# The first expert slots' table moved into the second to last head pair, and the last pair's adds moved to VectorE

## The chip, the cores and the metric

The kernel runs on one core of one Trainium2 chip. The metric is the device time of one execution, in microseconds (us). The engines are TensorE (PE in the rows, its weight loads PEld), VectorE (DVE), ScalarE (ACT), GpSimd (POOL) and SyncE (SP), which issues most of the DMA transfers. GpSimd issues the indirect transfers (gathers and scatters).

## What is computed

Attention in which a query sees only keys of its own hash bucket (the signs of six projections), and then a mixture of experts with one expert for each token:

```python
scores = scale * np.matmul(q, k.transpose(0, 1, 3, 2))      # B=4, H=8, S=768, D=64
scores = np.where(q_bucket[..., None] == k_bucket[..., None, :], scores, -1e9)
attn = np.exp(scores - scores.max(-1, keepdims=True))
attn = attn / (attn.sum(-1, keepdims=True) + 1e-09)
x = np.matmul(attn, v).transpose(0, 2, 1, 3).reshape(3072, 512)
logits = x @ w_gate + modality_bias[modality_id]            # 8 experts
e_idx = np.argmax(logits, axis=1)
gate_w = softmax(logits)[np.arange(N), e_idx]
for e in range(8):
    mask = e_idx == e
    out[mask] = gate_w[mask, None] * (np.maximum(x[mask] @ w1[e], 0) @ w2[e])
```

## The kernel before

Attention is worked in 16 pairs of heads, i = 0 to 15; four pairs make a batch. A pair has six tiles of 128 keys, kt = 0 to 5. TensorE's instructions stand in the order in which the program's text issues them. That order is written out by hand as strings, one string for each kt: PLAN0 for pair 0, LAST for pair 15 and PLAN for the pairs between. The other engines' order comes from a scheduler. The letters that matter here:

- S is a score step: matmuls of L410 and L411, one exponential on ScalarE (L430 or L444) into a tile `pb`. After the last step of a key tile kt > 0 two adds (L447), one for each head h, sum the weights up in `sp`. They are GpSimd's, but in pair 15 those of h = 1 are VectorE's (CFG's `spd`).
- A weighs the values: 16 matmuls of L463 for two key tiles. Pair i's last A leaves its sums of all keys in `ut`.
- Q calls `sums(i - 1)`: eight matmuls (L486) that sum the previous pair's `sp` over the keys, and a copy or add of VectorE into `gs` (L489, L491). The adds of all six key tiles of pair i - 1 must be done for it. "sums(14)" below is the Q in pair 15. sums(15) is called by `finish(3)`, among the first matmuls of the experts.
- M prepares the next pair's masks (L344, L350 on TensorE, reduced on VectorE by L346, L352), T turns and takes signs of the pair after that (L220; VectorE's masks L231 and then L312), v sums the values up on GpSimd (`va`, L384 to L386).
- x and y take a step of `finish_x`: a tile of the last finished batch's x is transposed (four matmuls, L548), scaled on VectorE into `xs` (L550, two buffers) and stored to `x_d` in HBM by SP (L552). f, F, e and E are steps of `finish`, which divides by the sums, routes the tokens and has GpSimd scatter their numbers into the table `tab` in HBM (L784). For the third batch this scatter, six indirect transfers, runs in pairs 13 and 14.

The first expert block that is worked is known once three batches are routed. `early_slots` finds on VectorE where it lies (some 20 tiny instructions and `eslot`). SP reads `eslot` into a register and loads the rows `tb` of the table (L941). GpSimd makes `at` from them (L947) and gathers the tokens' x with four indirect transfers into `xg` (L949). TensorE transposes `xg` (L967, eight matmuls for the first two chunks of 128 columns, eight for the others), ScalarE copies (`xh`, L970), VectorE subtracts (`xl`, L974), and the first layer's matmuls `hps` start (L985 with `xh`, L986 with `xl`, L987 with `xh`, for each of four chunks c). The weights come as `raw`, ScalarE rounds them (`w`, L929), and VectorE or, for every second one of the first eight, GpSimd makes the rest (`w`, L933). The first eight transposes stand on TensorE behind pair 15's second A, the other eight behind its third.

Of the kernel before, what the change touches and what calls it, by code (L numbers as in the profile page):

```python
# [30 lines left out]
P = 128  # L31

GROUP = 2
PLAN = (
    "yMSTSTMSM",
    "STEeLfvxMAVSSMMTxfe",
    "eySMSMlARRQfMSFMyF",
    "SRMSeMSMx",
# [13 lines left out]
    "SevAVSSe",  # L52
    "eySSAQSy",
    "SSeS",
# [39 lines left out]
def attention(ctx, actx, tc, a, x_d, l_d, route=None, setup=None, before_last=None):  # L94
# [318 lines left out]
    def score(i):  # L413

        t = st[i]
        t["sp"] = spool.tile([P, 2, S], F32, name="sp")
        t["pb"] = [pbuf[(NT * i + kt) % NPB] for kt in range(NT)]

        banks = [0]

        def bank(shape):
            banks[0] += 1
            if i == NPR - 1 and banks[0] % 2:
                return ps_m.tile(shape, F32, name="psm")
            return ps_s.tile(shape, F32, name="pss")

        def main(kt, h):
            sp = bank([P, MAIN])
            scores(t, sp, h, kt, COLS[0])
            marks["p"] = nc.scalar.activation(t["pb"][kt][:, h, 0:MAIN], sp, AF.Exp, scale=0.125).ins  # L430

        if i == 0:
            for kt in range(NT):
                main(kt, 0)
                yield
        for kt in range(NT):
            pb = t["pb"][kt]
            for h in range(int(i == 0), 2):
                main(kt, h)
                yield  # L440
            sp = bank([P, 2, REST])
            for h in range(2):
                scores(t, sp[:, h], h, kt, COLS[1])
            nc.scalar.activation(pb[:, :, MAIN:S], sp, AF.Exp, scale=0.125)  # L444
            if kt > 0:
                for h in range(2):
                    marks["add"] = (nc.vector if h and i in CFG["spd"] else nc.gpsimd).tensor_tensor(out=t["sp"][:, h], in0=(t["pb"][0] if kt == 1 else t["sp"])[:, h], in1=pb[:, h], op=ALU.add).ins  # L447
            yield
# [137 lines left out]
    with tc.manual_schedule(engines={mybir.EngineType.PE}):  # L586
# [23 lines left out]
        for i in range(NPR):  # L610
# [8 lines left out]
            for kt in range(NT):  # L619
                if i == NPR - 1 and kt == 1:  # L620
                    before_last(ps_x.tile([P, MAIN], F32, name="psx"))
                if i == NPR - 1 and kt < 3:
                    next(xs, None)
                    next(xs, None)
                for c in (PLAN0 if i == 0 else LAST if i == NPR - 1 else PLAN)[kt]:
# [15 lines left out]
                    elif c == "V":  # L641
                        vsums(i)
                    elif c == "Q":
                        if i > 0:
# [4 lines left out]
                    elif c == "l":  # L649
                        if i + 1 < NPR:  # L650
                            load_v(i + 1)
                    elif c == "F" and i % 4 == 0 or c == "f" and i % 4 == 1:
                        next(fins, None)
                    elif c == "e" and i % 4 >= 2 or c == "E" and i == NPR - 2:
                        next(fins, None)
                    elif c == "x" and i % 4 == 2 or c == "y" and i % 4 == 3:
                        next(xs, None)
                        next(xs, None)
# [36 lines left out]
def router(ctx, tc, a, x_d, tab):  # L695
# [136 lines left out]

    def early_slots(sp):
        out = const.tile([P, 2, EARLY], I32, name="eslot")
# [50 lines left out]
def experts(ctx, tc, a, x_d, tab, out, ps_x, idents, fold, marks):  # L885
# [66 lines left out]
    def xprep(s, xg, dst):  # L952
# [11 lines left out]
        for c in range(4):  # L964
# [6 lines left out]
            if s == ("e", 0) and c == 1:  # L971
                after(marks["U", 4], tr.ins)
                after(marks["ut"], cp.ins)
            nc.vector.tensor_tensor(out=xl[:, c, 0:SL], in0=tp[:, 0:SL], in1=xh[:, c, 0:SL].bitcast(F32), op=ALU.subtract)  # L974
            if c % 2:
# [221 lines left out]
def body(tc, a, out):  # L1197
# [4 lines left out]
    with ExitStack() as ctx, ExitStack() as actx:  # L1202
        route, early_slots, late_slots, setup = router(ctx, tc, a, x_d, tab)
        finish, finish_x, ps_x, idents, fold, marks = attention(ctx, actx, tc, a, x_d, None, route, setup, lambda sp: eslot.append(early_slots(sp)))
        actx.close()
# [40 lines left out]
```

## Time and profile before

| | us |
|---|---|
| median of three runs | 759.83 (759.24 to 761.26) |
| the profiled execution, its own time | 760.22 |
| its span, first to last instruction | 758.1 |
| TensorE busy in it | 738.9 |
| VectorE, GpSimd, ScalarE busy | 499.9, 440.9, 363.8 |

The profiled execution is one run of the program. Its own time is 2.1 us longer than its span, and 0.39 us longer than the median. Pair 14 runs from about 411 to 430 us in it, pair 15 to 458 us, and the experts from there to the end.

### The profile page before, as it was taken

What the parts mean: (1) busy time and instruction counts of PE and PEld (TensorE: products, weight loads), DVE (VectorE), ACT (ScalarE), POOL (GpSimd) and SP (SyncE); (2) the same over time, 40 slices, a digit from 0 to 9 for tenths busy, and PEclk for the clock granted to TensorE, in tenths of its full rate; (3) what the DMA queues carried; (4) which work ended last, traced back from release to release, by engine and by line L of the source; (5) the groups of instructions that cost most, each with busy time, mean ns of one, the idle gap of its engine ahead of it and who ended that gap; (6) DMA issues with size and microseconds to landing.
All of it is one profiled execution on the core that took longest, in us unless ns stands there. A gap on an engine that the chain in (4) does not pass through costs nothing.

```text
span 758.1 us, 12219 instructions
## 1 busy us (share of the span) xinstructions
PE 738.9 (97%) x4308; PEld 523.4 (69%) x4308; DVE 499.9 (66%) x878; ACT 363.8 (48%) x649; POOL 440.9 (58%) x339
## 2 busy tenths in 40 slices
PE   6899999999999999999999999999999999999995
PEld 3556576566666657666666656888888877788884
DVE  6997779789877887977987877654343442334423
ACT  5446565555555555556465454343343432424333
POOL 8598779769888769887869984712222202202011
PEclk9999999999999999999999999999999999999998
DMA  9464455345676435664324163556544764434332
GB/s 187 116 142 109 113 122 140 83 106 116 111 131 162 105 91 133 121 157 124 92 69 85 61 199 112 115 207 185 159 137 139 250 214 147 141 123 139 96 113 82
DMA packets 105832, 99.26 MB, mean 131 GB/s; under 512 B 62594, under 2 KB 82978, under 8 KB 105760
## 3 DMA queue, kind: packets, MB, share of 16 engines
q1 hardware_dynamic: 99616, 83.79, 43.6%
q0 software_dynamic: 4832, 12.94, 4.9%
q10 hardware_dynamic: 1312, 1.65, 0.9%
q8 instruction: 36, 0.59, 0.4%
q14 instruction: 36, 0.29, 0.2%
HBM read 59.33 MB, written 12.94 MB: 95 GB/s over the span
## 4 chain that ended last, share of the span: by engine, by line
PE 81%; issue 9%; DMA 3%; POOL 2%; SPq 1%; DVE 1%; ACT 1%; POOLq 0%; ACTq 0%
PE psu L463 17%; PE pss L410 9%; PE pss L411 8%; PE psm L344 5%; PE hps L985 5%; PE hps L986 5%; PE hps L987 5%; PE yps L1026 4%; PE yps L1027 4%; PE yps L1028 4%; PE psm L350 3%; PE psx L303 2%; PE psx L486 2%; PE psx L548 2%; PE psu L220 1%
## 5 line engine op out<-in xcount | busy, mean ns | idle before, releaser
L447 POOL TENSOR_TENSOR sp<-sp,pb 128x768 f32<-128x768 f32 x124 | 225.3, 1851 | 14.1 <-ACT pb L444 13.4
L346 DVE TENSOR_REDUCE mx<-psm 128x1 f32<-128x512 f32 x192 | 130.0, 687 | 22.2 <-PE psm L344 19.1
L430 ACT ACTIVATE pb<-pss 128x512 f32<-128x512 f32 x186 | 111.5, 600 | 58.7 <-PE pss L411 50.2
L463 PE MATMUL psu<-pb,vt 128*64 128x512 f32 (+1 forms) x768 | 136.1, 497 | 0.0
L933 DVE TENSOR_TENSOR w<-raw,w 128x1024 fp32r<-128x1024 f32 x52 | 66.9, 1287 | 97.9 <-ACT w L929 97.3
L463 PEld LDWEIGHTS psu<-pb,vt 128*64 128x64 f32 x768 | 51.3, 137 | 70.6 <-issue 60.9
L929 ACT CAST w<-raw 128x1024 fp32r<-128x1024 f32 x56 | 58.5, 1047 | 81.4 <-PE yps L1028 76.7
L444 ACT ACTIVATE pb<-pss 128x512 f32<-128x512 f32 x93 | 55.6, 598 | 82.3 <-PE pss L411 80.0
L1096 POOL DMA_INDIRECT out<-y,tb x25 | 24.6, 984 | 104.1 <-ACT y L1095 100.4
L447 POOL TENSOR_TENSOR sp<-pb,pb 128x768 f32<-128x768 f32 x31 | 56.2, 1835 | 45.2 <-ACT pb L444 45.2
L1026 PE MATMUL yps<-w,hl 128*128 128x512 f32 x200 | 79.5, 397 | 0.0
L1027 PE MATMUL yps<-w,hh 128*128 128x512 f32 x200 | 78.1, 391 | 0.0
L1028 PE MATMUL yps<-w,hh 128*128 128x512 f32 x200 | 78.0, 390 | 0.0
L949 POOL DMA_INDIRECT xg<-x_d,tb x17 | 18.4, 1084 | 98.1 <-DMA tb<-tab 94.4
L985 PE MATMUL hps<-xh,w 128*128 128x496 f32 x192 | 74.4, 388 | 0.0
L986 PE MATMUL hps<-xl,w 128*128 128x496 f32 x192 | 73.8, 384 | 0.0
L987 PE MATMUL hps<-xh,w 128*128 128x496 f32 x192 | 73.8, 384 | 0.0
L410 PE MATMUL pss<-m_0g,s_0g 128*128 128x512 f32 (+1 forms) x186 | 69.2, 372 | 0.0
L991 DVE SCALAR_TENSOR_TENSOR hl<-hps,hh 128x496 fp32r<-128x496 f32 x48 | 32.4, 674 | 53.0 <-ACT hh L990 52.9
L352 DVE TENSOR_REDUCE mx<-psm 128x2 f32<-128x512 f32 x96 | 66.1, 688 | 1.0
L410 PE MATMUL pss<-m_1g,s_1g 128*128 128x512 f32 (+1 forms) x186 | 65.7, 353 | 0.2 <-ACT pb L430 0.2
L990 ACT ACTIVATE hh<-hps 128x496 fp32r<-128x496 f32 x48 | 28.1, 585 | 78.5 <-PE hps L987 76.1
(267 smaller groups left out, 1419.7 us busy)
## 6 DMA issues: line engine op xcount, KB each, us to landing
raw<-moe_w SPq DMA_DIRECT2D x56, 512.0 KB
vt<-v SPq DMA_DIRECT2D x16, 384.0 KB
qk<-q SPq DMA_DIRECT2D x31, 192.0 KB
qk<-k SPq DMA_DIRECT2D x31, 192.0 KB
x_d<-xs SPq DMA_DIRECT2D x18, 256.0 KB
tw<-moe_w SPq DMA_DIRECT2D x2, 2048.0 KB
m_0g<-m_0g SPq DMA_DIRECT2D x16, 192.0 KB
s_0g<-s_0g SPq DMA_DIRECT2D x16, 192.0 KB
```

The source lines that it names most:

```text
L346: marks["m"] = nc.vector.tensor_reduce(out=mx[:, qt + j, hi, 0:1], in_=mp, axis=AX.X, op=ALU.max).ins
L410: nc.tensor.matmul(out, t["s1"][h][:, ks], t["m1"][h][:, cs], start=True, stop=False)
L430: marks["p"] = nc.scalar.activation(t["pb"][kt][:, h, 0:MAIN], sp, AF.Exp, scale=0.125).ins
L447: marks["add"] = (nc.vector if h and i in CFG["spd"] else nc.gpsimd).tensor_tensor(out=t["sp"][:, h], in0=(t["pb"][0] if kt == 1 else t["s ...
L463: marks["u", kt] = nc.tensor.matmul(t["u"][part][64 * h:64 * h + 64, 0:w], t["v"][:, h, kt], t["pb"][kt][:, h, COLS[part]], start=False, s ...
L933: (nc.gpsimd if n < 8 and n % 2 else nc.vector).tensor_tensor(out=lo, in0=r, in1=hi.bitcast(F32), op=ALU.subtract)
L985: nc.tensor.matmul(hps, lo[:, c, fs], xh[:, c, 0:SL], start=(c == 0), stop=False)
L986: nc.tensor.matmul(hps, hi[:, c, fs], xl[:, c, 0:SL], start=False, stop=False)
L987: nc.tensor.matmul(hps, hi[:, c, fs], xh[:, c, 0:SL], start=False, stop=(c == 3))
L1026: nc.tensor.matmul(yps[g], hl[fc][:, gs], hi[:, fb], start=(fc == 0), stop=False)
L1027: nc.tensor.matmul(yps[g], hh[fc][:, gs], lo[:, fb], start=False, stop=False)
L1028: nc.tensor.matmul(yps[g], hh[fc][:, gs], hi[:, fb], start=False, stop=(fc == 7))
```

## The change

Four edits:

1. `early_slots` is called in pair 14 at kt = 1, not in pair 15, and its numbers stand in a tile `esp` of SBUF, not in a PSUM bank.
2. All six tiles of the third batch's x are transposed and stored in pair 14; before, the last three were in pair 15.
3. In pair 15 VectorE does nine of the ten adds; before, it did five. The two adds of the last key tile stand behind the subtraction `xl` of chunk 1.
4. In pairs 1 to 13 the Q stands at the end of kt = 1's scores and ahead of the T there; before, it stood behind the first A, in kt = 2. Pairs 14 and 15 keep its place (the letter q).

```diff
@@ -30,11 +30,12 @@
 CFG = dict(spd=(15,), fxs=3, wy=(0.3, 0.71), hpf=0, he=0, hn=0, hm=0, avp=(1, 2, 3, 4, 5, 6), avs=(2,), early=2, w3=(0, 0.9), x3=(0, 1), nmd=1, man=(), man0=2, hpo=0, hpe=0, p0=(0, 1), p1=(0, 0.25), p2=(0, 0.4), p3=(0.4, 0.9), s0=4, rc='DDDD', rq=(1, 2), tq=(3, 3, 1, 1, 0, 0), wh=(0.5, 0.78), ws=(0.78, 1.05), n2=2, psx=2, psm=2, pss=2, npb=6, ut=8, qk=4, v=2, wm=(0, 0.9), wf=(0.04, 1.02), wx=(0.3, 0.71), sub="DPPD", fx='D', fx3='R', raw=4, wp=7, LS=4, LL=7, pn=8, rv=(0,), rs='DDPP', r1=(0, 0.5), r2=(0, 1), avg=1, fub=2, fd=2, pm=(), fj=0, fxe=1.0)
 P = 128
 
+EARLY_AT = 1
 GROUP = 2
 PLAN = (
     "yMSTSTMSM",
-    "STEeLfvxMAVSSMMTxfe",
-    "eySMSMlARRQfMSFMyF",
+    "STEeLfvxMAVSSMMQTxfe",
+    "eySMSMlARRqfMSFMyF",
     "SRMSeMSMx",
     "SFfEMSfMRSMF",
     "fSMRSMMEBABSe",
@@ -50,7 +51,7 @@
 LAST = (
     "SySS",
     "SevAVSSe",
-    "eySSAQSy",
+    "eySSAqSy",
     "SSeS",
     "SSS",
     "SSASe",
@@ -444,7 +445,8 @@
             nc.scalar.activation(pb[:, :, MAIN:S], sp, AF.Exp, scale=0.125)
             if kt > 0:
                 for h in range(2):
-                    marks["add"] = (nc.vector if h and i in CFG["spd"] else nc.gpsimd).tensor_tensor(out=t["sp"][:, h], in0=(t["pb"][0] if kt == 1 else t["sp"])[:, h], in1=pb[:, h], op=ALU.add).ins
+                    marks["add"] = (nc.vector if i == NPR - 1 and (h or kt > 1) else nc.gpsimd).tensor_tensor(out=t["sp"][:, h], in0=(t["pb"][0] if kt == 1 else t["sp"])[:, h], in1=pb[:, h], op=ALU.add).ins
+                    marks["add", kt, h] = marks["add"]
             yield
 
     def weigh():
@@ -617,8 +619,8 @@
             if i % 4 == 2 and i > 4:
                 xs = finish_x(i // 4 - 1, 0, NT)
             for kt in range(NT):
-                if i == NPR - 1 and kt == 1:
-                    before_last(ps_x.tile([P, MAIN], F32, name="psx"))
+                if i == NPR - 2 and kt == EARLY_AT:
+                    before_last()
                 if i == NPR - 1 and kt < 3:
                     next(xs, None)
                     next(xs, None)
@@ -640,7 +642,7 @@
                         vadds(i)
                     elif c == "V":
                         vsums(i)
-                    elif c == "Q":
+                    elif c == "Q" and i < NPR - 2 or c == "q" and i >= NPR - 2:
                         if i > 0:
                             sums(i - 1)
                     elif c == "L":
@@ -653,7 +655,7 @@
                         next(fins, None)
                     elif c == "e" and i % 4 >= 2 or c == "E" and i == NPR - 2:
                         next(fins, None)
-                    elif c == "x" and i % 4 == 2 or c == "y" and i % 4 == 3:
+                    elif c == "x" and i % 4 == 2 or c == "y" and (i % 4 == 3 or i == NPR - 2):
                         next(xs, None)
                         next(xs, None)
         for _ in avs:
@@ -830,7 +832,8 @@
         nc.vector.tensor_reduce(out=r, in_=sel, axis=AX.X, op=ALU.add)
         nc.vector.tensor_scalar(out=out[:, 1], in0=r, scalar1=float(DUMMY), scalar2=None, op0=ALU.add)
 
-    def early_slots(sp):
+    def early_slots():
+        sp = const.tile([P, 96], F32, name="esp")
         out = const.tile([P, 2, EARLY], I32, name="eslot")
         nb, cu, cx, r = (sp[:, 8 * j:8 * j + 8] for j in range(1, 5))
         above(run[(B - 1) % 2], 0, sp, nb)
@@ -971,7 +974,10 @@
             if s == ("e", 0) and c == 1:
                 after(marks["U", 4], tr.ins)
                 after(marks["ut"], cp.ins)
-            nc.vector.tensor_tensor(out=xl[:, c, 0:SL], in0=tp[:, 0:SL], in1=xh[:, c, 0:SL].bitcast(F32), op=ALU.subtract)
+            sub = nc.vector.tensor_tensor(out=xl[:, c, 0:SL], in0=tp[:, 0:SL], in1=xh[:, c, 0:SL].bitcast(F32), op=ALU.subtract)
+            if s == ("e", 0) and c == 1:
+                for h in range(2):
+                    after(marks["add", NT - 1, h], sub.ins)
             if c % 2:
                 yield
 
@@ -1201,7 +1207,7 @@
     eslot = []
     with ExitStack() as ctx, ExitStack() as actx:
         route, early_slots, late_slots, setup = router(ctx, tc, a, x_d, tab)
-        finish, finish_x, ps_x, idents, fold, marks = attention(ctx, actx, tc, a, x_d, None, route, setup, lambda sp: eslot.append(early_slots(sp)))
+        finish, finish_x, ps_x, idents, fold, marks = attention(ctx, actx, tc, a, x_d, None, route, setup, lambda: eslot.append(early_slots()))
         actx.close()
         runner, tabs, conditional, yp, late_area, tiny = experts(ctx, tc, a, x_d, tab, out, ps_x, idents, fold, marks)
         r = runner()
```


What this does to the order of GpSimd's instructions in pairs 14 and 15: the rows from pair 14's kt = 2 on, first before. `pb_183` to `pb_186` are the weights of key tiles 2 to 5, `pb_181` and `pb_182` those of 0 and 1, "x2" the two heads.

```order
L447 TENSOR_TENSOR sp<-sp,pb_183 128x768 x2
L447 TENSOR_TENSOR sp<-sp,pb_184 128x768 x2
L447 TENSOR_TENSOR sp<-sp,pb_185 128x768 x2
L447 TENSOR_TENSOR sp<-sp,pb_186 128x768 x2
L447 TENSOR_TENSOR sp<-pb_181,pb_182 128x768
L947 TENSOR_SCALAR at<-tb 128x4
L949 DMA xg<-x_d,at 128x512 x4
L447 TENSOR_TENSOR sp<-sp,pb_183 128x768
```

And now, the same stretch (line numbers are up to six higher in the changed kernel):

```order
L387 TENSOR_TENSOR va_5100<-va_5100,va_5101 128x128
L950 TENSOR_SCALAR at<-tb 128x4
L448 TENSOR_TENSOR sp<-sp,pb_183 128x768 x2
L448 TENSOR_TENSOR sp<-sp,pb_184 128x768 x2
L448 TENSOR_TENSOR sp<-sp,pb_185 128x768 x2
L952 DMA xg<-x_d,at 128x512 x4
L448 TENSOR_TENSOR sp<-sp,pb_186 128x768 x2
L448 TENSOR_TENSOR sp<-pb_181,pb_182 128x768
L936 TENSOR_TENSOR w<-raw,w 128x1024 x2
```

The gathers have moved ahead of pair 14's last two adds, and `at` ahead of six more; the four adds of pair 15 that stood behind the gathers are gone from GpSimd.

VectorE at the end of pair 15, before, from the first add of that pair to the `gs` of sums(15):

```order
L447 TENSOR_TENSOR sp<-pb_181,pb_182 128x768
L491 TENSOR_TENSOR gs<-gs,psx 128x384
L447 TENSOR_TENSOR sp<-sp,pb_183 128x768
L447 TENSOR_TENSOR sp<-sp,pb_184 128x768
L447 TENSOR_TENSOR sp<-sp,pb_185 128x768
L933 TENSOR_TENSOR w<-raw,w 128x1024
L447 TENSOR_TENSOR sp<-sp,pb_186 128x768
L974 TENSOR_TENSOR xl<-psx,xh 128x496 x2
L933 TENSOR_TENSOR w<-raw,w 128x1024
L974 TENSOR_TENSOR xl<-psx,xh 128x496 x2
L491 TENSOR_TENSOR gs<-gs,psx 128x384
```

And now:

```order
L448 TENSOR_TENSOR sp<-pb_181,pb_182 128x768
L493 TENSOR_TENSOR gs<-gs,psx 128x384
L448 TENSOR_TENSOR sp<-sp,pb_183 128x768 x2
L448 TENSOR_TENSOR sp<-sp,pb_184 128x768 x2
L448 TENSOR_TENSOR sp<-sp,pb_185 128x768 x2
L936 TENSOR_TENSOR w<-raw,w 128x1024
L977 TENSOR_TENSOR xl<-psx,xh 128x496 x2
L448 TENSOR_TENSOR sp<-sp,pb_186 128x768 x2
L936 TENSOR_TENSOR w<-raw,w 128x1024
L977 TENSOR_TENSOR xl<-psx,xh 128x496 x2
L493 TENSOR_TENSOR gs<-gs,psx 128x384
```

The adds are two for each key tile, and the last two stand between the first and the second pair of `xl`. On TensorE the matmuls of sums(15) stand behind nine of the experts' matmuls, before behind seven.

TensorE in pair 1 around the Q, before:

```order
L350 MATMUL psm<-s_1g_116,m_1g_114 128x256 x2
L220 MATMUL psu_884<-qk,zst 32x384
...
L457 MATMUL psu_912<-lone,vs_193 128x256
L463 MATMUL psu_911<-pb_181,vt 64x512 x2
L463 MATMUL psu_912<-pb_181,vt 64x256 x2
L463 MATMUL psu_911<-pb_182,vt 64x512 x2
L463 MATMUL psu_912<-pb_182,vt 64x256 x2
L486 MATMUL psx<-sp,ones 32x384 x4
L350 MATMUL psm<-s_0g_115,m_0g_113 128x256 x2
```

And now:

```order
L351 MATMUL psm<-s_1g_116,m_1g_114 128x256 x2
L488 MATMUL psx<-sp,ones 32x384 x4
L221 MATMUL psu_891<-qk,zst 32x384
L221 MATMUL psu_890<-qk,zst 32x384 x2
L221 MATMUL psu_891<-qk,zst 32x384 x2
L221 MATMUL psu_890<-qk,zst 32x384 x2
```

The sums have moved from behind the A to ahead of the signs (L220, now L221), so that the signs, and the masks that VectorE makes of them, come behind them.

On SP the load of `tb`, which stood behind all six stores of the third batch's x, now stands behind two of them and ahead of four. It waits for the last scatter into the table.

## Rows read from the trace of the kernel before

**Rows 1.** Busy time of each engine, the page's first part.

```profile
PE 738.9 (97%) x4308; PEld 523.4 (69%) x4308; DVE 499.9 (66%) x878; ACT 363.8 (48%) x649; POOL 440.9 (58%) x339
```

**Rows 2.** The chain of work that ended last, shares by engine.

```profile
PE 81%; issue 9%; DMA 3%; POOL 2%; SPq 1%; DVE 1%; ACT 1%; POOLq 0%; ACTq 0%
```

**Rows 3.** Timeline of TensorE, 438 to 465 us: start, duration, instruction, [idle before it].

```profile
438.78 2.80 PE L463 MATMUL psu<-pb,vt 128*64 128x512 f32 x16
...
441.51 0.85 PE L486 MATMUL psx<-sp,ones 128*32 128x384 f32 x8
...
450.00 0.22 PE L967 MATMUL psx<-identr,xg 128*128 128x128 f32 x1
...
452.93 4.49 PE L463 MATMUL psu<-pb,vt 128*64 128x512 f32 x16
...
457.35 0.87 PE L967 MATMUL psx<-identr,xg 128*128 128x128 f32 x8
...
458.06 0.46 PE L985 MATMUL hps<-xh,w 128*128 128x496 f32 x1
...
460.58 0.49 PE L986 MATMUL hps<-xl,w 128*128 128x496 f32 x1
```

**Rows 4.** The gathers' line L949, who waited for them (us, times).

```profile
  PEld psx L967: 2.1, 3
...
DMA to landing us min/median/max: 5.1/6.3/7.3
```

**Rows 5.** Windows: busy time of each engine; PEclk is the granted clock.

```profile
16.00:18.00 2.00, 0.00 (x0) 0.00 (x0) 1.90 (x4) 1.94 (x6) 1.92 (x3) 1.00 1.10 217
...
454.00:456.00 2.00, 2.00 (x10) 0.77 (x8) 1.38 (x3) 1.64 (x2) 1.92 (x2) 0.50 0.13 48
```

**Rows 6.** Timeline of GpSimd, 416 to 470 us.

```profile
423.47 14.35 POOL L447 TENSOR_TENSOR sp<-sp,pb 128x768 f32<-128x768 f32 x8
...
441.37 0.23 POOL L947 TENSOR_SCALAR at<-tb 128x4 int32<-128x4 int32 x1 [1.51 <-DMA tb<-tab]
...
443.79 1.72 POOL L949 DMA_INDIRECT xg<-x_d,at  x1 [0.30 <-issue]
...
447.29 1.17 POOL L949 DMA_INDIRECT xg<-x_d,at  x1 [0.30 <-issue]
...
457.41 5.75 POOL L933 TENSOR_TENSOR w<-raw,w 128x1024 fp32r<-128x1024 f32 x2
```

**Rows 7.** Timeline of SP, the load of the table's rows.

```profile
439.11 0.42 SPq L941 DMA_DIRECT2D tb<-tab  x1
```

**Rows 8.** Timeline of VectorE, 436 to 464 us.

```profile
438.34 2.34 DVE L447 TENSOR_TENSOR sp<-pb,pb 128x768 f32<-128x768 f32 x1
...
443.70 0.96 DVE L447 TENSOR_TENSOR sp<-sp,pb 128x768 f32<-128x768 f32 x1 [0.72 <-ACT pb L444]
...
453.81 1.24 DVE L974 TENSOR_TENSOR xl<-psx,xh 128x496 fp32r<-128x496 f32 x2
...
455.67 2.87 DVE L933 TENSOR_TENSOR w<-raw,w 128x1024 fp32r<-128x1024 f32 x1 [0.62 <-ACT w L929]
```

**Rows 9.** Costliest groups, the page: busy, mean ns of one, idle before.

```profile
L933 DVE TENSOR_TENSOR w<-raw,w 128x1024 fp32r<-128x1024 f32 x52 | 66.9, 1287 | 97.9 <-ACT w L929 97.3
```

**Rows 10.** Timeline of ScalarE, the weights' rounding.

```profile
453.63 2.00 ACT L929 CAST w<-raw 128x1024 fp32r<-128x1024 f32 x2
```

**Rows 11.** The last scatters' line L784, six in 395 to 425 us.

```profile
L784 POOL DMA_INDIRECT tab<-rec,posi x6: 958/969/972, 402.8 to 412.6; - x6
...
DMA to landing us min/median/max: 3.7/6.8/10.2
```

**Rows 12.** Timeline of VectorE in pair 1.

```profile
68.81 0.56 DVE L489 COPY gs<-psx 128x384 f32<-128x384 f32 x1
...
69.28 0.68 DVE L352 TENSOR_REDUCE mx<-psm 128x2 f32<-128x512 f32 x1
```

**Rows 13.** Timeline of TensorE in pair 1.

```profile
70.19 0.39 PE L344 MATMUL psm<-s_1g,m_1g 128*128 128x512 f32 x1
```

## The prediction

> **What bounds the kernel now.** I read the busy times first: TensorE works in 97% of the span, no other engine in more than 66% [rows 1]. The chain of waits says the same: TensorE holds 81% of it [rows 2]. An edit therefore gains only where TensorE stands still or runs slowly. Behind the start there is one such place, which the timelines of TensorE and GpSimd show: the gather of the first expert block.
>
> TensorE starts the first transposes of the gathered tokens at 450.00, and is through with that round when the last A starts, at 452.93 [rows 3]. It lost 2.1 us there in three waits for the gathers' transfers [rows 4]. Without them the round takes about what the second one takes, 0.8 us (0.71 from its start to the next instruction). GpSimd explains the lateness: SP asked for the table's rows at 439.11 [rows 7], `at` followed at 441.37, and the fourth gather ended at 447.29 + 1.17 = 448.46 [rows 6], with 5.1 to 7.3 us to landing [rows 4].
>
> Right behind the wait TensorE's granted clock fell to 0.50, that is 1.2 instead of 2.4 GHz [rows 5]. The A there takes 457.35 - 452.93 = 4.42 us; the same 16 matmuls took 441.51 - 438.78 = 2.73 in pair 15's first A [rows 3]. So the place costs 2.1 + 1.7 = 3.8 us. In 16 to 18 us TensorE did nothing at all, and the clock stayed at 1.00 [rows 5]: an idle time is not always followed by the low clock.
>
> The sum is made against the profiled execution, 760.22 us, which is 0.39 above the median of 759.83. A measurement of this kernel can tell about 0.3% from no change, 2.3 us.
>
> **Gathers earlier (edits 1 and 2): the place's 3.8 us are removed.** The early table needs only counts that stand in pair 14. SP's load of the rows then waits for the last scatter only. That was issued at 412.6, and the scatters land in 3.7 to 10.2 us [rows 11], so between 416.3 and 422.8. From SP's load to `at` it was 441.37 - 439.11 = 2.26 us [rows 6, 7], so `at` starts at 418.6 to 425.1, where GpSimd reaches it at 423.5, when the adds of kt = 2 began before [rows 6]. I take 423.8 for its end. The stores of x behind the load on SP are late by up to 4 us, and with them the two `xs` buffers and TensorE's transposes in pair 14; I count nothing for it, since the wait that comes next covers it.
>
> **The new wait: sums(14).** Pair 14's last two adds now stand behind the gathers on GpSimd, and TensorE's sums(14) need them; in TensorE's order all that is left of pair 15 stands behind those sums. Before, GpSimd did eight adds in 14.35 us, 1.79 each, to 437.82, and TensorE came at 441.51 [rows 3, 6], so they had 3.7 us to spare. Now: 423.8 + 6 x 1.79 = 434.5; four gathers. Each took 1.17 in the last row and 0.30 before it, and 1.72 where VectorE was adding [rows 6, 8]: 5.9 us in all at 1.17, 8.1 at 1.72. I take 5.9, as VectorE then mostly reads PSUM, which makes 440.4; 0.3 more and 2 x 1.79 give 444.3. TensorE comes at some 441 to 442, so it waits 2 to 3 us, and sums(14) start 2.8 us later than before (2.4 to 5).
>
> From sums(14) on TensorE's work is the same up to the gathered transposes, 450.00 - 441.51 = 8.49 us [rows 3], and the tokens have landed long since: the last gather ends at 440.4, and 7.3 more is 447.7, against 444.3 + 8.5 = 452.8. Then 0.8 for the round, 2.73 for the A, 0.71 for the second round [rows 3]. The first `hps` starts at 444.3 + 8.49 + 0.8 + 2.73 + 0.71 = 457.0, before at 458.06: **-1.1 us**. The gain of 3.8 goes mostly into the wait before sums(14).
>
> **VectorE's adds (edit 3).** VectorE's add takes 0.96 us alone [rows 8], against GpSimd's 1.79. Those of kt = 2 to 4 lie under TensorE's scores. The two of kt = 5 stand between the first and second pair of `xl`, with a split of `w` behind them. Nine `hps` matmuls (0.225 each by the seven in 458.06 to 460.58, less sums(15)' 0.78) stand ahead of sums(15), so TensorE would reach the tenth, which needs chunk 2's `xl`, at 457.0 + 2.0 + 0.8 = 459.8. Before it reached that point, two matmuls further than where it stood at 460.58 [rows 3], at 461.03.
>
> VectorE's side: the first pair of `xl` ended at 455.05 [rows 8] behind a round that ended at 452.93. The round now ends at 453.6, and no add stands right ahead of `xl`, so 455.2. ScalarE has the weights for GpSimd's split ready at about 454.6, the first of the two casts from 453.63 [rows 10], and GpSimd's split took 2.9 [rows 6]. VectorE's adds beside a GpSimd operation took 2.34, not 0.96: that one began at 438.34, and ended when GpSimd's add that had just begun was done, and 0.96 had gone by [rows 8]. The low end, no overlap: 455.2 + 2 x 0.96 + 1.29 for the split [rows 9] + 0.62 for one `xl` (half of 1.24, [rows 8]) = 459.0, and TensorE's 459.8 decides. The high end, an add of 2.34, one of 0.96, a split of 2.87 and 0.65: 462.0. A case between, in which the first add waits until GpSimd's split ends at 457.5: 457.5 + 1.92 + 1.29 + 0.62 = 461.3. The two begin within half a microsecond of each other (455.2 and 454.6), and no row says which comes first, so I take the middle of 459.8 and 461.3, 460.5. Against 461.03 that is **-0.5 us** (-1.2 to +1.0). The Trainium skill ("SBUF — State Buffer", section "Who interferes with whom") says that whichever of the two issues first holds the shared ports for its whole instruction, and that the other blocks; by it the middle case, 461.3 or +0.3, is the one to expect, and the row of 2.34 agrees.
>
> **The sums ahead of the signs (edit 4).** Nothing is added. In each of 13 pairs the eight matmuls of 0.85 us [rows 3] go ahead of the signs, and `gs`, 0.47 on VectorE from its start to the next instruction [rows 12], with them. GpSimd's adds of the pair before are done by then. The signs, masks and L312 come up to 0.85 later, less the 0.47 that `gs` no longer takes behind them, so the reduction that started at 69.28 and frees a bank at 69.96 comes up to 0.4 later, and TensorE's L344 at 70.19 [rows 13] has 0.23 to spare: 0.15 us a pair at most there, 2 us in 13 pairs. On the other side the waits for `gs` in `finish` shrink, by less than 0.1 in some five pairs. I take **+0.3** (-0.4 to +2).
>
> **Sum.** 760.22 - 0.5 + 0.3 = 760.0. (The -1.1 lies inside the -0.5: TensorE arrives earlier and waits for `xl`.)
>
> **Rivals.**
>
> *Faster: sums(14) don't wait.* If GpSimd's adds and gathers took less, or TensorE came later to the sums, the 3.8 us would be kept. GpSimd would have to be done by about 441.5, 2.8 us before my sum; its eight adds were as short as they get in the row. A partial form, in which the sums wait 1 us less and no lock falls on `xl`, has TensorE there at 458.8, -2.2 us, and gives 758.3; the whole 3.8 gives 756.4. Chance 0.25 for more than 2.3 us.
>
> *Slower: VectorE's chain in the 13 pairs.* If the slack of 0.23 us is not there in most pairs, the later signs push each pair by the whole 0.38: 13 x 0.38 = 4.9, and with -0.5 that is 764.6. It becomes decisive from 0.2 us a pair. For it: VectorE works without a gap at that place; against it: TensorE has score steps to do at any time there, and none of its rows shows a wait. Chance 0.15.
>
> *Slower: the low clock comes back.* The new wait of 2 to 3 us before sums(14) can be followed by 1.2 GHz, as the one at 450 was and that at 16 us was not [rows 5]. It costs 1.7 us at the price of the A; VectorE's `xl` then waits less, so the net is +0.8 and the time 760.8; with a second one behind sums(15) it is 762.5. Chance 0.25, of which 0.1 above 762.1. The Trainium skill ("TensorE: Matmul & The Clock Gate", section "What's actually happening") has the engine fall back to 1.2 GHz after idle time; by it this case is likely, and the forecast 760.8.
>
> *Nothing happens,* because GpSimd stays as late as it was in the gathers: it doesn't, as `at` is ahead of six adds. Less than 0.05.
>
> **Chances.** My forecast, within 2.3 us of before (757.5 to 762.1), 0.47 with the mild forms of the clock; faster 0.26; slower 0.27. The range reaches from 756.6, the rival with most of the 3.8 us kept, to 763.6, between the clock's 762.5 and the chain's 764.6.
>
> **What the profile would show.** `at` ends near 424, and the gathers at 434 to 441, with no wait of the transposes for `xg`. TensorE idle 2 to 3 us before sums(14), released by GpSimd's adds, at 443 to 446. The A behind the transposes takes 2.73 us at clock 1.00. The first `hps` at 457, and a short wait of chunk 2's for VectorE. The pairs 1 to 13 keep their length to 0.1 us. I am wrong if sums(14) start before 442.5, if the 13 pairs move by more than 1 us in sum, or if `xl` of chunk 2 is later than 462.

## The result, and the profile after

The changed kernel takes 764.57 us (median of five runs, 762.71 to 767.25), the one before 759.24 in the five runs beside it (757.82 to 761.26). The ratio is 1.008, 95% interval 1.0065 to 1.0096: slower by 0.8%. The profiled run took 764.57, its span is 762.7, where 758.1 stood before.

The page's busy times and the shares of the chain of waits, after:

```profile
PE 739.0 (97%) x4308; PEld 525.2 (69%) x4308; DVE 501.6 (66%) x882; ACT 363.0 (48%) x649; POOL 430.9 (56%) x335
...
PE 77%; issue 10%; POOL 3%; DMA 3%; DVE 3%; SPq 2%; ACT 1%; POOLq 0%; ACTq 0%; DVEq 0%
```

TensorE does the same work as before [rows 1] in a longer span, and its share of the chain fell from 81% [rows 2] to 77%. VectorE's share rose from 1 to 3%. So the reader looks for a place where TensorE waits for VectorE. TensorE's timeline has it (start, duration, instruction, idle time before it with what ended it):

```profile
426.05 0.50 PE L345 MATMUL psm<-s_0g,m_0g 128*128 128x512 f32 x1 [2.65 <-DVE mx L347]
...
444.43 0.85 PE L488 MATMUL psx<-sp,ones 128*32 128x384 f32 x8
...
452.93 0.79 PE L970 MATMUL psx<-identr,xg 128*128 128x128 f32 x8
...
453.65 2.80 PE L465 MATMUL psu<-pb,vt 128*64 128x512 f32 x16
...
457.08 0.47 PE L991 MATMUL hps<-xh,w 128*128 128x496 f32 x1
...
463.41 1.51 PE L488 MATMUL psx<-sp,ones 128*32 128x384 f32 x8 [4.07 <-DVE xl L977]
```

Three things are to be seen, against [rows 3]. The transposes L970 have no wait any more, and the 16 matmuls of the A behind them run from 453.65 until the next transposes, which came at 456.38 in the trace: 2.73 us where it took 4.42. The first `hps` starts at 457.08, before at 458.06. And there are two waits that were not there: 2.65 us in pair 14, for VectorE's L347, and 4.07 us ahead of sums(15), for VectorE's `xl`. The sums themselves then take 1.51 us instead of 0.85. The granted clock says why, in windows (behind the window and its length stands TensorE's busy time; the granted clock is the third number from the right):

```profile
452.00:456.00 4.00, 4.00 (x30) 2.30 (x28) 2.92 (x5) 2.81 (x5) 0.25 (x1) 1.00 0.41 98
...
460.00:462.00 2.00, 0.00 (x0) 0.00 (x0) 2.00 (x1) 0.00 (x0) 1.69 (x1) 0.98 0.66 255
...
462.00:464.00 2.00, 0.59 (x4) 0.20 (x8) 1.94 (x3) 0.00 (x0) 0.00 (x0) 0.50 0.28 12
...
466.00:468.00 2.00, 2.00 (x8) 1.65 (x7) 0.38 (x3) 0.00 (x0) 0.00 (x0) 0.50 0.60 230
```

TensorE does nothing from 460 to 462, and from 462 to 468 it works at 0.50, 1.2 GHz. At 452 to 456, where [rows 5] had the half clock before, it is at 1.00.

What VectorE did meanwhile (timeline; its rows come from two windows, the second add is also part of the x2 row):

```profile
424.70 0.69 DVE L552 TENSOR_TENSOR xs<-psx,rin 128x512 f32<-128x512 f32 x1 [2.96 <-DMA x_d<-xs]
...
441.29 4.98 DVE L448 TENSOR_TENSOR sp<-pb,pb 128x768 f32<-128x768 f32 x1 [0.78 <-ACT pb L445]
...
454.28 1.26 DVE L977 TENSOR_TENSOR xl<-psx,xh 128x496 fp32r<-128x496 f32 x2 [1.08 <-ACT xh L973]
...
455.45 4.02 DVE L448 TENSOR_TENSOR sp<-sp,pb 128x768 f32<-128x768 f32 x2
...
456.32 3.16 DVE L448 TENSOR_TENSOR sp<-sp,pb 128x768 f32<-128x768 f32 x1
...
459.40 3.37 DVE L936 TENSOR_TENSOR w<-raw,w 128x1024 fp32r<-128x1024 f32 x1
...
462.69 1.24 DVE L977 TENSOR_TENSOR xl<-psx,xh 128x496 fp32r<-128x496 f32 x2
```

And GpSimd:

```profile
423.94 0.23 POOL L950 TENSOR_SCALAR at<-tb 128x4 int32<-128x4 int32 x1 [0.84 <-DMA tb<-tab]
...
440.06 3.62 POOL L448 TENSOR_TENSOR sp<-sp,pb 128x768 f32<-128x768 f32 x2
...
443.64 1.81 POOL L448 TENSOR_TENSOR sp<-pb,pb 128x768 f32<-128x768 f32 x1
...
455.75 2.92 POOL L936 TENSOR_TENSOR w<-raw,w 128x1024 fp32r<-128x1024 f32 x1 [10.30 <-ACT w L932]
...
459.35 2.34 POOL L936 TENSOR_TENSOR w<-raw,w 128x1024 fp32r<-128x1024 f32 x1 [0.69 <-ACT w L932]
```

The two adds of the last key tile take 4.02 us instead of 1.92. The first one is through after 0.87; the second begins at 456.32 and ends at 459.48, 0.81 us after GpSimd's first split has ended (455.75 + 2.92 = 458.67). VectorE's own split starts at 459.40, 0.05 us behind GpSimd's second one, ends at 462.77, and had to wait for that one's end at 461.69. So chunk 2's `xl`, which the prediction had end at 461.3 in its middle case and at 462.0 at the latest, starts at 462.69 and ends at 463.35. The sums(15) waited for it themselves: the PSUM bank `psx` that they write is freed when `xl` has read it (the releaser in TensorE's row). The add from 441.29 shows the same at full length: 4.98 us, until all three of GpSimd's adds that stand back to back from 440.06 are done at 445.45.

The wait in pair 14 comes from SP's queue:

```profile
421.85 0.42 SPq L944 DMA_DIRECT2D tb<-tab  x1
...
422.33 5.97 SPq L554 DMA_DIRECT2D x_d<-xs  x4
```

The load of the table's rows waited on SP for the last scatter until 421.85; the four stores of x behind it went out from 422.33 on, and the `xs` of 424.70 had waited 2.96 us for a buffer. How long TensorE waits there differs from one execution to the next: the traces of the seven runs below with the same order on SP, up to that place, have 0.23 to 1.35 us there. The 2.65 us are this execution's and not a fixed price of the edit.

### The profile page after: what moved, and what is told of

It is laid out like the page before. It is cut to its first block, busy times and chain, and to the rows that moved or that the text cites. A ratio compares the mean times of both kernels' runs of the same rounds, so it can differ in the third digit from the quotient of the medians.

```text
span 762.7 us, 12235 instructions
## 1 busy us (share of the span) xinstructions
PE 739.0 (97%) x4308; PEld 525.2 (69%) x4308; DVE 501.6 (66%) x882; ACT 363.0 (48%) x649; POOL 430.9 (56%) x335
## 4 chain that ended last, share of the span: by engine, by line
PE 77%; issue 10%; POOL 3%; DMA 3%; DVE 3%; SPq 2%; ACT 1%; POOLq 0%; ACTq 0%; DVEq 0%
PE psu L465 15%; PE pss L411 8%; PE pss L412 8%; PE psm L345 5%; PE hps L991 5%; PE hps L993 5%; PE hps L992 5%; PE yps L1032 4%; PE yps L1033 4%; PE yps L1034 4%; PE psm L351 3%; PE psx L304 2%; PE psx L488 2%; PE psu L221 2%; PE psx L550 1%
## 5 line engine op out<-in xcount | busy, mean ns | idle before, releaser
L448 POOL TENSOR_TENSOR sp<-sp,pb 128x768 f32<-128x768 f32 x120 | 216.7, 1842 | 12.4 <-ACT pb L445 10.8
L347 DVE TENSOR_REDUCE mx<-psm 128x1 f32<-128x512 f32 x192 | 130.0, 687 | 21.9 <-PE psm L345 18.5
L465 PE MATMUL psu<-pb,vt 128*64 128x512 f32 (+1 forms) x768 | 134.4, 492 | 0.0
```

The lines of the kernel that those rows point to most:

```text
L347: marks["m"] = nc.vector.tensor_reduce(out=mx[:, qt + j, hi, 0:1], in_=mp, axis=AX.X, op=ALU.max).ins
L448: marks["add"] = (nc.vector if i == NPR - 1 and (h or kt > 1) else nc.gpsimd).tensor_tensor(out=t["sp"][:, h], in0=(t["pb"][0] if kt == 1 ...
L465: marks["u", kt] = nc.tensor.matmul(t["u"][part][64 * h:64 * h + 64, 0:w], t["v"][:, h, kt], t["pb"][kt][:, h, COLS[part]], start=False, s ...
```

## The experiments

Each kernel differs from the changed one by the edit shown, if not told otherwise. The changed kernel stands at 764.57 (ratio 1.008). Each ratio is to the kernel before on the same chip, whose median was 758.1 to 758.2 there.

**The last two adds on GpSimd.**

```diff
-... (nc.vector if i == NPR - 1 and (h or kt > 1) else nc.gpsimd) ...
+... (nc.vector if i == NPR - 1 and (h or kt > 1) and kt < NT - 1 else nc.gpsimd) ...
...
-            if s == ("e", 0) and c == 1:
-                for h in range(2):
-                    after(marks["add", NT - 1, h], sub.ins)
```

> The changed kernel with the last key tile's two adds of pair 15 given back to GpSimd, so that nothing but the split of w stands between the two pairs of xl on VectorE. Theory A (the loss is the wait of 4.07 us for chunk 2's xl, whose adds and split stand behind GpSimd's splits, and the half clock of some 2.6 us that follows it): the wait falls under 1.5 us, no half clock follows, and the time is about 758 us (757 to 760). Theory B (the loss is the wait of 2.65 us in pair 14 for the late stores of x): nothing changes there, and the time stays at 763 to 765. Theory C (the sums ahead of the signs lengthen the pairs): 763 to 765 too.

758.35 us, ratio 0.9996 (0.9985 to 1.0008): 6.2 us less. TensorE's wait before sums(15):

```profile
458.28 0.85 PE L488 MATMUL psx<-sp,ones 128*32 128x384 f32 x8 [0.39 <-DVE xl L977]
```

The clock stays at 1.00 behind it. In this order of the other work, the loss hung on where these two adds are done.

**The same two adds on VectorE, but ahead of the first xl.**

```diff
-            if s == ("e", 0) and c == 1:
-                for h in range(2):
-                    after(marks["add", NT - 1, h], sub.ins)
```

> The changed kernel without the rule that puts the last two adds behind xl of chunk 1: VectorE does them ahead of the first xl, at about 453.8 to 455.7, before GpSimd's first split begins at 455.75. Theory A: the adds take 0.96 each, and only the split of w is then held by GpSimd's split, to about 458.7, so chunk 2's xl ends near 460.5 and TensorE waits 1 us or less: 759 to 761 us. Theories B and C: 763 to 765.

758.96 us, ratio 1.0011 (1.0001 to 1.0022). The adds took 1.82 together, from 453.32, and TensorE waited 0.94. The adds are cheap; their place beside GpSimd's splits was not.

**GpSimd's first two splits given to VectorE.**

```diff
-(nc.gpsimd if n < 8 and n % 2 else nc.vector).tensor_tensor(out=lo, ...
+(nc.gpsimd if 3 < n < 8 and n % 2 else nc.vector).tensor_tensor(out=lo, ...
```

> The changed kernel with GpSimd's first two splits of w (the second and fourth) given to VectorE too: VectorE has more work, and nothing holds its ports there. Theory A: the two adds take 0.96 each and the split 1.2, chunk 2's xl begins at about 458.7, TensorE waits 0.5 us or less, no half clock: 758 to 760 us. Rival E (VectorE has simply too much to do between the two pairs of xl): the wait stays above 3 us and the time at 763 us or more.

757.27 us, ratio 0.9993 (0.998 to 1.0006), and TensorE has no wait before sums(15) at all. VectorE, in the changed kernel's own order:

```profile
453.88 1.82 DVE L448 TENSOR_TENSOR sp<-sp,pb 128x768 f32<-128x768 f32 x2
...
455.62 1.21 DVE L936 TENSOR_TENSOR w<-raw,w 128x1024 fp32r<-128x1024 f32 x1
...
456.76 1.24 DVE L977 TENSOR_TENSOR xl<-psx,xh 128x496 fp32r<-128x496 f32 x2
```

VectorE has two splits more than in the changed kernel, and the same adds, split and `xl` take 1.82, 1.21 and 1.24. So rival E is out: it was not VectorE's load but GpSimd's operations beside it.

**Stores of x issued by ScalarE.**

```diff
-marks["x", b] = (nc.scalar if b == B - 1 else nc.sync).dma_start( ...
+marks["x", b] = (nc.scalar if b >= B - 2 else nc.sync).dma_start( ...
```

> The changed kernel with the third batch's stores of x issued by ScalarE, so that they don't stand behind the table's load on SP. Theory A: the wait of 2.65 us in pair 14 goes, but TensorE then waits some 1.9 us before sums(14), since GpSimd's adds end at 443.7 as before; all behind it is 0.7 us earlier, with the same wait for xl: 763.5 to 764.5. Theory B: 2.65 us less, 762 us.

772.04 us, ratio 1.018 (1.0163 to 1.0197). Both theories missed. VectorE's and GpSimd's timelines tell why:

```profile
413.70 8.59 DVE L833 TENSOR_SCALAR eslot<-esp 128x2 int32<-128x2 f32 x1
```

```profile
413.26 0.96 POOL L786 DMA_INDIRECT tab<-rec,posi  x1 [0.30 <-issue]
...
414.24 3.56 POOL L448 TENSOR_TENSOR sp<-sp,pb 128x768 f32<-128x768 f32 x2
...
417.76 3.55 POOL L448 TENSOR_TENSOR sp<-pb,pb 128x768 f32<-128x768 f32 x2
...
421.27 0.98 POOL L385 TENSOR_TENSOR va<-vt 128x384 f32<-128x384 f32 x1
```

The last instruction of the early table, which writes two numbers for each of 128 partitions, took 0.17 us in the changed kernel at 413.02. Here it began at 413.70, under GpSimd's last scatter, and was held through four adds that follow one another until GpSimd's `va` ended at 422.25. Why the scatter held it here, and not in the changed kernel, where it also fell under one, no run shows. In the kernel before the same instruction read PSUM (edit 1 moved its numbers to SBUF), and an add of GpSimd did not hold it:

```profile
438.04 1.82 POOL L447 TENSOR_TENSOR sp<-pb,pb 128x768 f32<-128x768 f32 x1 [0.22 <-ACT pb L444]
...
438.15 0.16 DVE L831 TENSOR_SCALAR eslot<-psx 128x2 int32<-128x2 f32 x1
```

TensorE stood still for 8.63 us behind it. The wait for `xl` later on was there as well, 4.06. As a test of the stores the run says nothing.

**The table's load behind four stores instead of two** is the same question without that accident.

```diff
+            marks["x", b, tt] = marks["x", b]
...
-        nc.sync.dma_start(out=tb[:, 0:n], ...
+        ld = nc.sync.dma_start(out=tb[:, 0:n], ...
+        if s == ("e", 0):
+            after(ld.ins, marks["x", B - 2, 3])
```

> The changed kernel as it is, with the table's load behind four of the stores of x instead of two, and nothing else. Theory A: the wait of 2.65 us in pair 14 goes, TensorE waits for GpSimd's adds before sums(14) instead, and the wait of 4 us for xl stays: 763 to 764.5 us. Theory B (the wait in pair 14 is the loss): 761 to 762 us.

764.52 us, ratio 1.0078 (1.0049 to 1.0108). The wait of 2.65 us in pair 14 was 0.33 in this trace (0.23 to 1.35 in the seven others, without this edit), TensorE waited for GpSimd's adds in the midst of sums(14) instead, and the wait for `xl` was the same:

```profile
443.36 0.84 PE L488 MATMUL psx<-sp,ones 128*32 128x384 f32 x4 [0.50 <-POOL sp L448]
...
462.31 1.51 PE L488 MATMUL psx<-sp,ones 128*32 128x384 f32 x8 [4.06 <-DVE xl L980]
```

Theory B is out: with next to no wait in pair 14 the time stays. Most of that wait lay ahead of another. Not all: the wait before sums(15) ends 463.41 - 462.31 = 1.1 us earlier than in the changed kernel, and the last matmul stands 1.0 earlier, at 754.41. The time doesn't show it, because the stretch behind the last matmul was 0.9 longer in this execution.

**The sums of pairs 1 to 13 back behind the first A.**

```diff
-    "STEeLfvxMAVSSMMQTxfe",
-    "eySMSMlARRqfMSFMyF",
+    "STEeLfvxMAVSSMMTxfe",
+    "eySMSMlARRQfMSFMyF",
...
-    "eySSAqSy",
+    "eySSAQSy",
...
-                    elif c == "Q" and i < NPR - 2 or c == "q" and i >= NPR - 2:
+                    elif c == "Q":
```

> The changed kernel with the sums of pairs 1 to 13 back behind the first A. Theories A and B: within 1 us of the changed kernel, since the pairs kept their length in its trace (the third A of pair 13 stands 0.6 us later than before). Theory C: 2 us or more less, near 761.

761.95 us, ratio 1.0045 (1.0029 to 1.0062), 2.6 less: theory C's number. In the changed kernel's trace its reason isn't there. From pair 0's last A to pair 13's it took 408.77 - 58.33 = 350.44 us, and this run took 350.74. But that trace is the exception. The run with the two adds ahead of the first `xl`, in which these pairs are the same as in the changed kernel, is a usual one (the second group of rows):

```profile
58.33 2.80 PE L465 MATMUL psu<-pb,vt 128*64 128x512 f32 x16
...
408.77 2.80 PE L465 MATMUL psu<-pb,vt 128*64 128x512 f32 x16
```

```profile
57.95 2.80 PE L465 MATMUL psu<-pb,vt 128*64 128x512 f32 x16
...
203.83 0.50 PE L345 MATMUL psm<-s_1g,m_1g 128*128 128x512 f32 x1 [0.51 <-DVE mx L353]
...
313.40 0.50 PE L345 MATMUL psm<-s_1g,m_1g 128*128 128x512 f32 x1 [0.51 <-DVE mx L353]
...
409.66 2.80 PE L465 MATMUL psu<-pb,vt 128*64 128x512 f32 x16
```

There it took 351.70. The three traces with the sums in their old place (this run, the kernel before, edit 3 alone) have 350.22 to 350.74; the eleven with edit 4 have 350.44 to 352.33, the middle one 351.68. Pair by pair, edit 4 makes most pairs 0.1 to 0.3 us shorter; pair 10 is 0.77 longer in all eleven, and pairs 6, 7 and 11 are 0.6 to 0.8 longer in some executions and not in others. In the changed kernel's trace only pair 10 is. In pairs 6 and 10 the trace shows 0.51 us of it as a wait of TensorE for VectorE's mask reduction; the rest, pairs 7 and 11 too, is open. So edit 4 costs about 1.3 us in the middle execution.

The wait before sums(15) is again 4.07. The half clock behind it was shorter: from the end of the wait to the first L523 it took 467.81 - 461.55 = 6.26 us, in the changed kernel 470.52 - 463.41 = 7.11, 0.85 more. The wait ends 1.86 us earlier than in the changed kernel, in these two executions mainly because pair 14 had 0.79 in place of 2.65, which is chance. Of the 2.6 between the medians, an estimate from single executions gives edit 4 half, 1.3; the rest, and what sets the length of the half clock, is open.

**Edits 1, 2 and 4 without edit 3.**

```diff
-... (nc.vector if i == NPR - 1 and (h or kt > 1) else nc.gpsimd) ...
+... (nc.vector if i == NPR - 1 and h else nc.gpsimd) ...
...
-            if s == ("e", 0) and c == 1:
-                for h in range(2):
-                    after(marks["add", NT - 1, h], sub.ins)
```

> Edits 1, 2 and 4 without edit 3: the adds of pair 15 are shared as in the kernel before. Theory A (GpSimd's operations hold VectorE's adds and split between the two pairs of xl): no add stands between them, the wait for chunk 2's xl is 1 us or less, and the time is 757.5 to 759.5 us. Rival D (the gathers' early place itself costs, by the adds behind them and the wait in pair 14): 761 us or more.

762.97 us, ratio 1.0077 (1.0058 to 1.0096). Missed, and on the side of rival D. TensorE and VectorE:

```profile
459.32 1.32 PE L970 MATMUL psx<-identr,xg 128*128 128x128 f32 x8 [4.52 <-DVE xl L977]
```

```profile
445.86 7.04 DVE L448 TENSOR_TENSOR sp<-sp,pb 128x768 f32<-128x768 f32 x3
...
455.59 3.09 DVE L448 TENSOR_TENSOR sp<-sp,pb 128x768 f32<-128x768 f32 x1
```

With the adds shared as before, GpSimd adds right through pair 15, and VectorE's three adds take 7.04 us and its last one 3.09, which now stands ahead of `xl`. The second round of transposes waits 4.52 us for a bank that `xl` empties. So the early gathers need an edit of the adds, but not this order of them: what is common to both slow forms is a VectorE add held by GpSimd ahead of an `xl`.

**Edit 3 alone, on the kernel before** (the same two places of the diff).

> The kernel before with edit 3 alone (nine adds of pair 15 on VectorE, the last two behind xl of chunk 1). Theory A: the gathers' wait of 2.1 us and its half clock stay, and a wait of 2 to 4 us for chunk 2's xl is added, with or without a half clock behind it: 761 to 764.5 us. Rival D: edit 3 alone costs nothing, 758 to 759.5.

761.28 us, ratio 1.006 (1.0042 to 1.0079). Theory A's size, with one part of its reason wrong:

```profile
459.50 0.85 PE L487 MATMUL psx<-sp,ones 128*32 128x384 f32 x8 [3.80 <-DVE xl L975]
```

The transposes waited 0.33 and 0.36 us for the gathers, with no half clock behind, and the wait for `xl` is 3.80 with the half clock behind it. Edit 3 by itself brings the loss.

**Work for TensorE in the wait.** 18 matmuls of 496 columns, into a PSUM bank that nobody reads.

```diff
...
-                nc.tensor.matmul(hps, hi[:, c, fs], xl[:, c, 0:SL], start=False, stop=False)
+                mm = nc.tensor.matmul(hps, hi[:, c, fs], xl[:, c, 0:SL], start=False, stop=False)
+                if c == 2 and ("fill" not in marks):
+                    marks["fill"] = ps_y.tile([P, DM], F32, name="yps")
+                    for _ in range(18):
+                        fill = nc.tensor.matmul(marks["fill"][:, 0:SL], identr, xh[:, 0, 0:SL], ...)
+                        after(fill.ins, marks["h"])
+                    for q in marks["q", 15]:
+                        after(q, fill.ins)
+                marks["h"] = mm.ins
```

`marks["q", 15]` are the matmuls of sums(15).

> The changed kernel with 18 matmuls (496 columns, into a PSUM bank that nobody reads) added on TensorE ahead of the sums(15), about 4 us of work in the place of the wait of 4.07 us. It takes the idle time away and not the lateness of xl. If the half clock of 462 to 468 us is the price of that idle time, the granted clock stays at 1.00 there and the time is 2.0 to 2.8 us under the changed kernel's, near 762 us. If the half clock has another cause, it stays, and the time is 764.5 or more.

767.28 us, ratio 1.0132. The scheduler put a matmul that needs chunk 2's `xl` behind the first two of them, so the wait of 4.05 stayed and the others were added behind it. It decides nothing. With that matmul kept behind all 18 as well:

```diff
-                    for q in marks["q", 15]:
+                    for q in marks["q", 15] + [mm.ins]:
```

> As the run before with the 18 added matmuls, which left the wait in place because one matmul that needs chunk 2's xl stood between the first two and the others: that matmul now stands behind all 18, so that they fill the wait of some 4 us. If the half clock is the price of the idle time, the granted clock stays at 1.00 from 458 to 470 us and the time is 2.0 to 2.8 us under the changed kernel's, near 762 us. If it has another cause, the half clock stays and the time is 764.5 us or more.

762.34 us, ratio 1.005 (1.0036 to 1.0063). TensorE, and the windows:

```profile
457.71 4.25 PE L997 MATMUL yps<-xh,identr 128*128 128x496 f32 x18
...
462.44 0.85 PE L488 MATMUL psx<-sp,ones 128*32 128x384 f32 x8 [0.48 <-DVE xl L978]
```

```profile
456.00:460.00 4.00, 4.00 (x21) 3.35 (x21) 4.00 (x2) 2.25 (x5) 3.32 (x2) 1.00 0.29 75
...
462.00:464.00 2.00, 1.56 (x12) 0.83 (x12) 1.52 (x3) 0.00 (x0) 0.00 (x0) 1.00 0.42 101
...
466.00:468.00 2.00, 2.00 (x13) 1.18 (x14) 1.18 (x4) 0.35 (x1) 0.00 (x0) 1.00 0.09 35
```

The granted clock stays at 1.00, `xl` is as late as before against the first `hps`, and the time is 2.2 us less, although TensorE does 4 us of work for nothing. The half clock was the price of the idle time. From the end of the wait to L523 it is 467.55 - 462.44 = 5.11, with two `hps` matmuls (0.45) more than in the changed kernel; so the half clock took 7.11 - 4.66 = 2.45 there. The run with GpSimd's first splits on VectorE, which had no wait there, has 4.65 for the same matmuls. By that measure the half clock took 2.6 in the run with the table's load behind four stores, and 1.6 in three others (stores by ScalarE, sums in the old place, edit 3 alone), behind waits of 3.80 to 4.07.

**A version that beats both.** GpSimd's first two splits on VectorE, as above, and the table's load behind four stores:

> The changed kernel with GpSimd's first two splits given to VectorE (as the run that had no wait for xl), and with the table's load on SP behind four of the stores of x instead of two. The wait of 1.35 us in pair 14 goes; TensorE then waits before sums(14) until GpSimd's adds end near 443.5, so 0 to 0.7 us less than without: 756.5 to 757.5 us. If the wait in pair 14 had a price of its own, 755.5 to 756.

757.27 us, ratio 0.9995 (0.9979 to 1.0011): no less than without the second edit. TensorE waited 0.48 and 0.92 us for GpSimd's adds before and in the sums(14). And with the gathers behind pair 14's last two adds on GpSimd (each is put after `marks["add14"]`, the last of these adds):

> As the one before, and with the gathers behind pair 14's last two adds on GpSimd instead of ahead of them. Sums(14) no longer wait; the gathers end near 443.5 instead of 439.2 and land by 450, where TensorE comes at about 449: a wait of 0 to 1 us there. If the theory of two waits in a row on GpSimd (adds or gathers) is right, 1.5 to 2.5 us less than without: 754.5 to 756 us. If the landing is late instead, the gain is given back, and a half clock may follow: 757 to 758.5.

756.42 us, ratio 0.9977 (0.996 to 0.9993): 0.2% under the kernel before, and 0.85 us less than without the last edit, where 1.5 to 2.5 were expected; those two intervals overlap. TensorE and GpSimd:

```profile
442.57 0.85 PE L490 MATMUL psx<-sp,ones 128*32 128x384 f32 x8
...
451.07 0.79 PE L977 MATMUL psx<-identr,xg 128*128 128x128 f32 x8
...
455.22 0.47 PE L998 MATMUL hps<-xh,w 128*128 128x496 f32 x1
```

```profile
424.73 14.37 POOL L448 TENSOR_TENSOR sp<-sp,pb 128x768 f32<-128x768 f32 x8
...
443.17 0.95 POOL L957 DMA_INDIRECT xg<-x_d,at  x1 [0.30 <-issue]
```

Sums(14) don't wait, and neither do the transposes: the last gather ends at 444.12, 7 us ahead of them. The first `hps` starts at 455.22, 2.8 us earlier than before. Edit 4 is still in this version, and its pairs up to 13 took 352.33 us, 2.0 more than before's 350.37. The same version with the sums in their old place was not run.

## Why the prediction was wrong

Forecast: 760.0 in 756.6 to 763.6; measured 764.57, above the range, and slower where no change was forecast.

*Gathers earlier.* Right. The wait is gone and the clock is 1.00 under the A, 2.73 us. `at` ended at 424.17, forecast 423.8.

*Sums(14).* GpSimd's adds of pair 14 were done at 443.68, and the sums started at 444.43, forecast 444.3; the first `hps` stood at 457.08, forecast 457.0. That both agree is luck. TensorE did not wait there, because it had already lost 2.65 us in pair 14, for the stores of x behind SP's load. The prediction counted nothing for these, as the wait for the adds would cover them. It covered all but 444.43 - 443.68 = 0.75 us of this trace's 2.65.

*The term that failed is "VectorE's adds (edit 3)", -0.5 with a range of -1.2 to +1.0.* It took 460.5 for the tenth `hps`, the middle of 459.8 (no wait) and 461.3 (chunk 2's `xl` late by one split), with 462.0 at the high end; `xl` ended at 463.35. Later than 462 was the prediction's own sign of being wrong. The middle case let GpSimd's one split of 2.9 us hold the adds, and left VectorE's split at 1.29. The high end held one add and the split, each for the time of a row of before, 2.34 and 2.87. There were two splits of GpSimd, and each held one operation of VectorE to its end: ScalarE's next rounding ended at 458.17 + 1.11 = 459.28, GpSimd's second split began at 459.35, and it held VectorE's split for the whole of its 2.34. The adds' 4.02 and the split's 3.37 make 7.4 us, where the middle case had 2.3 + 1.92 + 1.29 = 5.5 and the high end 6.2. The Trainium skill ("SBUF — State Buffer", section "Who interferes with whom") gives the rule that the prediction quoted: who comes second waits for the other's whole instruction. The rows agree to 0.15 us in both cases: VectorE's add and split ended 0.81 and 1.08 us after GpSimd's splits, and take 0.96 and 1.21 alone. I had the rule, and in the middle case applied it to one instruction. The add at 441.29 goes beyond it: it was held through three.

The same term let sums(15) run while `xl` was late, and only the tenth `hps` wait. They waited too, so their 0.78 us came behind the wait. At the full clock the tenth `hps` would have started at 463.41 + 0.78 = 464.19, against 461.03 before: +3.2 where -0.5 was forecast. Smaller, and without effect on the result: the nine `hps` ahead were put at 0.225 each, but the seven of before take 460.58 - 458.06 - 0.78 = 1.74 us, 0.25 each; nine took 459.34 - 457.08 = 2.26, not 2.0.

*The half clock.* It was a rival with a chance of 0.25, tied to the wait before sums(14), net +0.8 (762.5 with a second one behind sums(15)), and not in the sum. It came behind the wait for `xl`, which was longer than any that I had reckoned with, and took 2.45. The row of 16 to 18 us, an idle time with no half clock behind it, was one execution's: in ten of the thirteen other traces, the changed kernel's among them, the clock is 0.50 for a stretch between 18 and 23 us.

*Edit 4.* +0.3 forecast (-0.4 to +2), and the pairs moving by more than 1 us in sum was a sign of being wrong. In the changed kernel's profiled execution they moved by 350.44 - 350.37 = 0.1, in the middle one of eleven by 1.3. The place was named rightly (the reduction that frees TensorE's bank), the size was not, and one trace was not enough to see it. The rival that rested on it gave 764.6, the measured time; that is chance, as the profiled execution lost its time elsewhere.

The sum as measured, in the profiled execution: TensorE was ready for sums(15) at 459.34, and before it reached the same point (two `hps` further) at 459.80 + 0.45 = 460.25, so -0.9; +4.07 for the wait; +2.45 for the half clock: +5.6. The last matmul of the program stands 5.6 later, 755.39 against 749.79. The execution is 4.35 longer (764.57 against 760.22), since the stretch behind the last matmul was 1 us shorter in this run, and the time outside the span 0.2 shorter. That stretch was 6.3 to 8.1 us in the fourteen traces; why it differs was not followed up.

## What to carry to other kernels

When work is moved from GpSimd to VectorE, list what GpSimd will do in the same microseconds, with the instruction that comes after the next one, and give VectorE's operation the rest of each one that it meets. A wait that is covered by a later one costs little, and its removal brings little: both ends of such a pair have to go, as in the last version. A stall of some 4 us on TensorE has a second price, the half clock behind it, here 1.6 to 2.6 us. And a term of some tenths in each of 13 pairs is not read from one execution: the changed kernel's own trace had 0.1 us where the middle one of eleven had 1.3.

## What the runs showed of the hardware that was not expected

VectorE can be held through several of GpSimd's instructions that follow each other without a gap. One add was held through three of GpSimd's adds (4.98 us for 0.96), and a VectorE instruction on two numbers a partition through four adds and a `va` (8.59 us for 0.17). It is not always so. In the kernel before [rows 6, 8] GpSimd's last add ended at 448.47 + 8.99 = 457.46, with its two splits right behind until 463.16, and VectorE's split from 455.67 was done at 458.54, 1.08 us after that add. What tells the two cases apart no run shows.

TensorE's clock behind a wait: 1.00 after the single waits of up to 2.65 us, 0.50 after those of 3.80, 4.05 to 4.07, 4.52 and 8.63 us, and 1.00 when the same 4 us were filled with matmuls whose result nobody reads. In the kernel before it was 0.50 after three waits that came one after another, 2.1 us in all [rows 4, 5].
